# Pieces of W2's products in idle row quarters of the score visits, v passes that wait, zeros in early pauses, and a new plan

## The chip, the cores and the metric

The kernel runs on one core of a Trainium2 chip. The metric is the device time of one execution in microseconds (us). The core has a matrix engine (TensorE, here PE, with its weight loads PEld), a vector engine (DVE), a scalar engine (ACT), a general engine (POOL) and the queue that issues most DMAs (SP). They run side by side and wait for each other through semaphores.

## The reference

A block with 2048 tokens of 640 features mixes attention and a dense layer by a gate. In short:

```
qkv = x @ wqkv                       # 640 -> 3 * 640, 32 heads of 20
p   = softmax(q @ k.T * 20 ** -0.5)  # per head, 2048 x 2048
a   = (p @ v) @ wo
h   = x @ w1 + b1                    # 640 -> 1536
b   = (h * tanh(softplus(h))) @ w2   # 1536 -> 640
g   = sigmoid(sum(x * gate_w))
out = g * a + (1 - g) * b
```

The scores are the bulk: 32 heads x 2048 x 2048 exponentials.

## The kernel before

**Tiles.** Queries go in four chunks (c) of 512, heads in eight groups (g) of four (j = 0 to 3), keys in 16 tiles (kt) of 128. A unit (c, g, kt, j) is a score block of 128 keys by 512 queries; there are 2048. A head has 20 features, padded to 32 rows, so the product of a unit uses one 32-row quarter of PE's array, quarter j. Products in different quarters run beside each other (`score_mms`, L1294). All other products use all 128 rows and are cut into four column quarters of 32 (`quarters`, L532; `pv`, L1539), or use the whole array (`v_task`, `v_pair_task`, L853 and L880).

**Steps.** The main loop makes one exponential per step on ACT (`emit_e`, L1321), over two units, or three where `third` allows it. In the same step PE gets the scores of two steps later (`emit_s`): a visit of two or three units, to which `x_block` may add one whose exponential DVE makes. DVE converts that score block to an integer whose bits are a half float (L1379) and makes two shifted copies for each set of four (`piece`, L1409); the copies are weighted by scaled values V made on POOL (`weigh`, L1435). Such a set of four is called a tile here. After the scores, PE does passes with v (`emit_pv`: four heads at once, into bank ACC) and products of a task.

**Tasks.** Projections of K, Q and V, W1 (`h_task`, ten products), W2 (`b_task`: twelve products of 320 columns for 128 tokens and half of the features, 32 such tasks) and W_o (`p_task`) are `Task` objects, in a list in order of due times. One task at a time is open; `put` issues its products one after the other into one bank of PSUM, and the last product starts its eviction (`finish`). Banks 0 to 2 and 3 to 5 hold the scores of even and odd steps. Bank 6 is ACC. Banks 7, 5 and 2 are shared (`FLEX`): a third unit, a block for DVE or an open task takes one.

**The plan.** Everything is ordered when the kernel is built. `Plan` keeps an estimated clock per engine; `Plan.add` puts an instruction on an engine's list, with a cost, and charges SWITCH when PE changes between the kinds S (scores), V (v passes and column-quartered tasks) and F. The loop's choices compare these clocks with some thirty constants. STRETCHES gives other values for them from a step on, in 35 stretches. SHADE is the planned cost of a shifted copy. The finished lists run on the chip in that order, with semaphores only where one engine needs another's result.

**The start.** PE does six products of zeros into bank 5 and 7 (L599), turns the first 256 tokens by products with a unit matrix (`turn` in `first_keys`, L801), projects Q and K of head group 0 for them (`project`, L620), turns the next 256 tokens, and does the first scores. ACT and DVE copy results out of PSUM between these (L789, L790).

Of the kernel before, what the change touches and what calls it, by code (L numbers as in the profile page):

```python
# [49 lines left out]
SWITCH = 0.1025  # L50
# [93 lines left out]
SHADE = 0.61  # L144


EARLY = 0.35
SOON = 0.0
# [3 lines left out]
    13: {"CALM": 12, "CROWD": 1.22, "EAGER": 73, "FMIN": 0.198, "LATER": 0.157, "ROOM": 2.755, "SOON": 0.205, "SPUN": 0.607, "THIRD": 0.945, "VMIN": 1.27, "XSLACK": 0.224},  # L152
    33: {"AHEAD": 29, "BEHIND": 26.388, "CALM": 12, "CROWD": 1.22, "EAGER": 73, "FMIN": 0.198, "LATER": 0.157, "OVER": 0.17, "ROOM": 2.755, "SOON": 0.205, "SPUN": 0.607, "THIRD": 0.938, "VMIN": 1.398, "XSLACK": 0.37},
    53: {"AHEAD": 29, "BEHIND": 26.388, "BUSY": 0.647, "CALLED": 4.748, "CALM": 12, "CROWD": 1.22, "EAGER": 73, "EARLY": 0.551, "FMIN": 0.198, "KEPT": 12, "LATER": 0.157, "MARGIN": 0.809, "OVER": 0.17, "ROOM": 2.352, "SLACK": 0.261, "SOON": 0.092, "SPUN": 0.607, "THIRD": 0.938, "VMIN": 1.274, "XSLACK": 0.527},
    75: {"AHEAD": 29, "BEHIND": 15.903, "BUSY": 0.62, "CALLED": 4.748, "CALM": 12, "CROWD": 1.042, "EAGER": 83, "EARLY": 0.551, "FMIN": 0.122, "KEPT": 11, "LATER": 0.157, "MARGIN": 0.809, "OVER": 0.17, "PATIENCE": 7.416, "ROOM": 2.352, "SLACK": 0.261, "SOON": 0.092, "SPUN": 0.607, "STREAM": 0.537, "THIRD": 0.938, "VMIN": 1.274, "XSLACK": 0.527},
    97: {"AHEAD": 29, "BEHIND": 15.903, "BUSY": 0.62, "CALLED": 4.748, "CALM": 12, "CROWD": 1.042, "EAGER": 83, "EARLY": 0.551, "FMIN": 0.122, "KEPT": 11, "LATER": 0.157, "MARGIN": 0.809, "OVER": 0.17, "PATIENCE": 7.416, "ROOM": 2.352, "SLACK": 0.261, "SOON": 0.092, "SPUN": 0.607, "STREAM": 0.537, "THIRD": 0.938, "VMIN": 1.274, "XSLACK": 0.527},
    119: {"AHEAD": 29, "BEHIND": 15.903, "BUSY": 0.62, "CALLED": 4.748, "CALM": 12, "CROWD": 1.042, "EAGER": 83, "EARLY": 0.551, "FMIN": 0.122, "KEPT": 11, "LATER": 0.157, "MARGIN": 0.809, "OVER": 0.127, "PATIENCE": 7.416, "ROOM": 2.352, "SLACK": 0.261, "SOON": 0.092, "SPUN": 0.607, "STREAM": 0.537, "THIRD": 0.938, "VMIN": 1.274, "XSLACK": 0.527},
    141: {"BEHIND": 24.559, "CALLED": 1.144, "EARLY": 0.264, "KEPT": 12, "OVER": 0.186, "SPUN": 0.579},
    163: {"AHEAD": 21, "BEHIND": 24.496, "CALLED": 1.144, "CROWD": 0.988, "EARLY": 0.17, "KEPT": 12, "MARGIN": 0.364, "OVER": 0.186, "PATIENCE": 7.069, "ROOM": 2.123, "SPUN": 0.579, "VMIN": 0.687, "XLATE": 9.675},
    185: {"AHEAD": 21, "BEHIND": 24.496, "CALLED": 1.144, "CROWD": 0.988, "EARLY": 0.17, "KEPT": 12, "MARGIN": 0.364, "OVER": 0.26, "PATIENCE": 7.069, "ROOM": 2.123, "SPUN": 0.579, "STREAM": 0.336, "VMIN": 0.687, "XLATE": 9.675},  # L160
    205: {"AHEAD": 25, "BEHIND": 35.465, "CALLED": 0.932, "CROWD": 0.9, "EARLY": 0.172, "KEPT": 12, "MARGIN": 0.029, "OVER": 0.26, "PATIENCE": 3.704, "ROOM": 2.123, "SPUN": 0.579, "STREAM": 0.401, "VMIN": 0.687, "XLATE": 6.805, "XSLACK": 0.455},
    226: {"AHEAD": 25, "BEHIND": 35.465, "CALLED": 0.932, "CROWD": 0.9, "EARLY": 0.172, "KEPT": 12, "MARGIN": 0.029, "OVER": 0.26, "PATIENCE": 3.704, "ROOM": 2.123, "SOON": 0.261, "SPUN": 0.579, "STREAM": 0.401, "VMIN": 0.687, "XLATE": 6.805, "XSLACK": 0.612},
    247: {"AHEAD": 30, "BEHIND": 35.465, "CALLED": 0.932, "CROWD": 1.967, "EARLY": 0.172, "FMIN": 0.388, "FREE": 0.17, "KEPT": 12, "LATER": 0.621, "MARGIN": 0.029, "OVER": 0.322, "PATIENCE": 3.704, "ROOM": 2.123, "SOON": 0.261, "SPARED": 2, "SPUN": 0.579, "STREAM": 0.365, "VMIN": 0.687, "XLATE": 6.805, "XSLACK": 0.57},
    269: {"CALLED": 8.383, "SPUN": 0.576, "XSLACK": 0.465},
    288: {"CALLED": 8.383, "NEED": 6, "SPUN": 0.576, "XSLACK": 0.562},
    309: {"BEHIND": 23.94, "BUSY": 0.781, "CALLED": 8.383, "NEED": 6, "OVER": 0.396, "SPUN": 0.576, "THIRD": 0.444, "XSLACK": 0.562},
    329: {},
    351: {"BEHIND": 22.936, "BUSY": 0.732, "CROWD": 1.732, "EARLY": 0.305, "LOAD": 0.675, "OVER": 0.179, "PATIENCE": 2.889, "ROOM": 2.208, "VMIN": 0.705, "XLATE": 7.367, "XSLACK": 0.617},
    371: {"CALM": 7, "EARLY": 0.394, "MARGIN": 1.067, "SOON": 0.284, "STREAM": 0.467, "THIRD": 0.922},
    393: {"BEHIND": 28.654, "FMIN": 0.064, "LOAD": 0.638, "PATIENCE": 8.55, "VMIN": 0.653, "XSLACK": 0.487},  # L170
    413: {"MARGIN": 1.061, "SPUN": 0.615, "THIRD": 1.024, "XSLACK": 0.623},
    432: {"BUSY": 0.709, "CROWD": 0.989, "EARLY": 0.406, "FMIN": 0.123, "LATER": 0.297, "LOAD": 0.551, "MARGIN": 1.18, "OVER": 0.152},
    454: {"AHEAD": 38, "BUSY": 0.519, "CROWD": 0.989, "EAGER": 173, "EARLY": 0.406, "FMIN": 0.123, "LATER": 0.297, "LOAD": 0.551, "MARGIN": 1.161, "OVER": 0.152, "SPUN": 0.614, "STREAM": 0.359, "THIRD": 1.328, "VMIN": 1.002},
    474: {"AHEAD": 38, "BUSY": 0.807, "CALLED": 0.617, "CROWD": 0.989, "EAGER": 173, "EARLY": 0.406, "FMIN": 0.123, "LATER": 0.562, "LOAD": 0.551, "MARGIN": 1.161, "OVER": 0.152, "SPUN": 0.588, "STREAM": 0.359, "THIRD": 1.386, "VMIN": 1.939, "XSLACK": 0.252},
    494: {"BEHIND": 26.661, "BUSY": 0.707, "EAGER": 167, "MARGIN": 1.1, "PATIENCE": 3.566, "SPUN": 0.577, "STREAM": 0.513, "VMIN": 0.663, "XSLACK": 0.781},
    514: {},
    536: {"BUSY": 0.585, "CALLED": 2.393, "EARLY": 0.384, "FMIN": 0.098, "FREE": 0.232, "LOAD": 0.545, "MARGIN": 0.445, "PATIENCE": 6.193, "SLACK": 0.245, "STREAM": 0.457, "VMIN": 1.484, "XLATE": 7.039, "XSLACK": 0.513},
    556: {"SPARED": 1, "SPUN": 0.709, "STREAM": 0.531},
    577: {"BEHIND": 22.355, "EAGER": 146, "EARLY": 0.229, "LOAD": 0.461, "MARGIN": 1.156, "OVER": 0.132, "SPARED": 2, "SPUN": 0.709, "STREAM": 0.531, "XLATE": 9.211},
    598: {"BEHIND": 22.355, "EAGER": 63, "EARLY": 0.229, "FREE": 0.05, "KEPT": 15, "LOAD": 0.461, "MARGIN": 1.156, "NEED": 3, "OVER": 0.132, "SPARED": 2, "SPUN": 0.685, "STREAM": 0.531, "THIRD": 0.482, "VMIN": 0.813, "XLATE": 8.949},  # L180
    618: {"SPARED": 2, "THIRD": 0.433},
    639: {"BEHIND": 33.829, "BUSY": 0.336, "EAGER": 128, "SOON": 0.138, "SPARED": 2, "THIRD": 0.545, "XSLACK": 0.736},
    659: {"BEHIND": 33.719, "BUSY": 0.336, "CROWD": 1.058, "EAGER": 56, "FMIN": 0.095, "FREE": 0.212, "KEPT": 9, "LOAD": 0.71, "OVER": 0.155, "PATIENCE": 8.654, "SLACK": 0.168, "SOON": 0.138, "SPARED": 2, "SPUN": 0.63, "THIRD": 0.545, "XLATE": 2.946, "XSLACK": 0.366},
    680: {"BUSY": 0.499, "CROWD": 1.717, "LATER": 0.593, "MARGIN": 1.084, "NEED": 6, "OVER": 0.173, "PATIENCE": 8.859, "SPARED": 1, "SPUN": 0.559},
    702: {"BUSY": 0.71, "CALLED": 2.994, "EAGER": 176, "EARLY": 0.4, "FMIN": 0.091, "LATER": 0.47, "LOAD": 0.734, "ROOM": 2.176, "SPUN": 0.633, "XSLACK": 0.653},
# [12 lines left out]


class Plan:  # L200
# [1934 lines left out]
```

## Time and profile before

| | before |
|---|---|
| time, median of 3 runs | 744.35 us (743.04 to 745.58) |
| the profiled execution's own time | 744.41 us |
| its span, first to last instruction | 742.5 us |
| busy PE / DVE / ACT / POOL | 721.6 / 692.5 / 722.5 / 366.6 us |
| exponentials on ACT (L1321) | 736, 700.3 us busy |

A page of the profile gives the busy time of each engine, the chain of work that ended last, and groups of instructions by line: out<-in, the count, then busy time and mean duration in ns, then the idle time of the engine before them and what ended it. Consecutive instructions overlap by their latency, so the mean duration is longer than the step from one to the next. In a row of the timeline the first number is the start, the second the time from the first start to the last end of instructions merged into the row. In a row of waits the numbers are the total, the count and the longest.

### The profile page before, as it was taken

What the parts mean: (1) busy time and instruction counts of PE and PEld (TensorE: products, weight loads), DVE (VectorE), ACT (ScalarE), POOL (GpSimd) and SP (SyncE); (2) the same over time, 40 slices, a digit from 0 to 9 for tenths busy, and PEclk for the clock granted to TensorE, in tenths of its full rate; (3) what the DMA queues carried; (4) which work ended last, traced back from release to release, by engine and by line L of the source; (5) the groups of instructions that cost most, each with busy time, mean ns of one, the idle gap of its engine ahead of it and who ended that gap; (6) DMA issues with size and microseconds to landing.
All of it is one profiled execution on the core that took longest, in us unless ns stands there. A gap on an engine that the chain in (4) does not pass through costs nothing.

```text
span 742.5 us, 25540 instructions
## 1 busy us (share of the span) xinstructions
PE 721.6 (97%) x11013; PEld 272.2 (37%) x11016; DVE 692.5 (93%) x1203; ACT 722.5 (97%) x767; POOL 366.6 (49%) x705
## 2 busy tenths in 40 slices
PE   8999999999999999999999999999999999999996
PEld 4333333332333333332333334443333333433343
DVE  3799999999999998999899999999999999999985
ACT  6999999999999999999999999999999999999995
POOL 3303333062357635454234682668548766765531
PEclk9999999999999999999999999999999999999999
DMA  9312413212231324236321323131142121211111
GB/s 208 90 31 68 97 58 87 67 50 68 80 95 44 98 78 135 76 88 188 95 58 51 91 68 99 56 90 50 45 108 59 56 82 55 82 38 42 41 32 49
DMA packets 85125, 56.67 MB, mean 76 GB/s; under 512 B 22116, under 2 KB 80988, under 8 KB 85004
## 3 DMA queue, kind: packets, MB, share of 16 engines
q1 hardware_dynamic: 82636, 54.47, 26.3%
q8 instruction: 89, 1.46, 0.9%
q10 hardware_dynamic: 2256, 0.47, 0.3%
q14 instruction: 32, 0.26, 0.1%
q0 software_dynamic: 112, 0.01, 0.1%
HBM read 41.31 MB, written 12.83 MB: 73 GB/s over the span
## 4 chain that ended last, share of the span: by engine, by line
PE 45%; ACT 34%; DVE 15%; POOL 3%; DMA 1%; issue 1%; POOLq 0%
ACT ETS L1321 33%; PE PS L1294 16%; PE PS L1539 13%; PE PS L532 13%; DVE LN L1379 5%; DVE LN L1409 3%; PE PS L880 2%; POOL HB L1059 2%; DVE REG L1379 1%; DVE U L1058 1%; DVE HB L1019 1%; PE PS L620 1%; POOL U L1057 1%; DMA W2R<-in_B_w_dram 1%; DVE U L1062 1%
## 5 line engine op out<-in xcount | busy, mean ns | idle before, releaser
L1321 ACT ACTIVATE ETS<-PS 128x1024 bf16<-128x1024 f32 (+1 forms) x736 | 700.3, 1099 | 5.1 <-PE PS L1294 3.4
L1294 PE MATMUL PS<-QT,KT 32*128 32x512 bf16 (+1 forms) x2126 | 294.9, 377 | 9.9 <-ACT ETS L1321 6.4
L1379 DVE TENSOR_SCALAR LN<-PS 128x512 int16<-128x512 f32 x412 | 273.1, 681 | 11.2 <-PE PS L1294 10.4
L1435 POOL TENSOR_SCALAR VS<-V_all 128x84 bf16<-128x84 bf16 x278 | 156.0, 561 | 94.9 <-PE PS L1539 60.0
L1294 PEld LDWEIGHTS PS<-QT,KT 32*128 32x128 bf16 x2126 | 75.4, 91 | 233.6 <-ACT ETS L1321 180.5
L1539 PE MATMUL PS<-ETS,V_all 128*21 128x512 bf16 (+1 forms) x1564 | 145.5, 375 | 0.0
L1409 DVE TENSOR_SCALAR LN<-LN 128x2048 int16<-128x2048 int16 x192 | 138.8, 727 | 4.5 <-PE PS L1539 4.3
L1059 POOL TENSOR_TENSOR HB<-U,HB 128x128 bf16<-128x128 f16 x192 | 97.0, 539 | 86.1 <-DVE U L1058 86.1
L1603 POOL TENSOR_TENSOR QT<-OUNG,BCT 128x128 bf16<-128x128 f32 x124 | 60.8, 521 | 110.0 <-DMA BCT<-SUMS 110.0
L532 PE MATMUL PS<-XB,REG 128*32 128x256 bf16 (+1 forms) x1800 | 87.8, 296 | 0.5 <-DVE LN L1379 0.3
L1539 PE MATMUL PS<-LN,VS 128*21 128x512 f16 (+1 forms) x884 | 83.1, 378 | 0.2 <-DVE LN L1409 0.2
L532 PE MATMUL PS<-W2R,HB 128*32 128x320 bf16 x1536 | 76.0, 301 | 0.6 <-DVE LN L1379 0.4
L1539 PEld LDWEIGHTS PS<-ETS,V_all 128*21 128x21 bf16 x1564 | 37.8, 90 | 49.6 <-issue 40.7
L532 PEld LDWEIGHTS PS<-XB,REG 128*32 128x32 bf16 x1800 | 41.1, 95 | 28.6 <-issue 19.4
L1057 POOL TENSOR_SCALAR U<-REG 128x256 f16<-128x256 f32 x72 | 35.3, 515 | 27.4 <-ACT REG L1043 26.3
L532 PEld LDWEIGHTS PS<-W2R,HB 128*32 128x32 bf16 x1536 | 35.5, 96 | 25.9 <-issue 13.1
L1379 DVE TENSOR_SCALAR REG<-PS 128x512 int16<-128x512 f32 x60 | 40.1, 680 | 1.5 <-PE PS L1294 1.5
L1539 PE MATMUL PS<-LN,V_all 128*21 128x512 f16 (+1 forms) x424 | 40.2, 375 | 0.0
L532 PE MATMUL PS<-XB,WOQ 128*32 128x512 bf16 (+2 forms) x440 | 35.6, 382 | 0.2
L1539 PEld LDWEIGHTS PS<-LN,VS 128*21 128x21 bf16 x884 | 20.7, 89 | 41.0 <-issue 25.3
L532 PE MATMUL PS<-WOQ,QT 128*32 128x320 bf16 (+1 forms) x672 | 33.7, 301 | 1.2 <-DVE REG L1379 0.5
L1019 DVE TENSOR_TENSOR HB<-PS,B1F 128x512 bf16<-128x512 f32 x48 | 32.6, 680 | 1.0 <-PE PS L532 1.0
(117 smaller groups left out, 537.6 us busy)
## 6 DMA issues: line engine op xcount, KB each, us to landing
REG<-in_B_w_dram SPq DMA_DIRECT2D x36, 320.0 KB, 3.2
BCT<-SUMS SPq DMA_DIRECT2D x31, 256.0 KB
OT<-QT SPq DMA_DIRECT2D x30, 128.0 KB, 2.6
W2R<-in_B_w_dram SPq DMA_DIRECT2D x12, 320.0 KB, 5.0
QT<-QS SPq DMA_DIRECT2D x28, 128.0 KB, 4.0
KT<-KS SPq DMA_DIRECT2D x28, 128.0 KB
KS<-LN SPq DMA_DIRECT2D x16, 128.0 KB, 4.1
QS<-WOQ SPq DMA_DIRECT2D x16, 120.0 KB
```

The costliest lines, as they stand in the source:

```text
L532: last = e.matmul(to[at + j:at + j + n, :], w[:, j:j + n], x, start=start, stop=stop, tile_position=(0, at + j))
L880: return lambda e, bank: e.matmul(PS[:, bank, i * n:(i + 1) * n], xt(t // 4)[:, f, t % 4 * P:(t % 4 + 1) * P], WV[:, f, g * HD:g * HD + n] ...
L1019: ev = dve(lambda e: e.tensor_tensor(hb, PS[:, bank, :].rearrange("p (i t) -> p i t", i=2), bias, ALU.add), [last, *b1f, *guarded, *b_read ...
L1057: lift = lambda e, at: e.tensor_scalar(A[:, at], U[:, at], LIFT, LIFT, ALU.mult, ALU.add)
L1059: last = lambda e, at: e.tensor_tensor(h[:, at], A[:, at], h[:, at], ALU.mult)
L1294: op = pl.add("pe", lambda e, to=to, g=real(g), tile=tile, j=j, cols=cols, c=c, of_q=of_q: e.matmul(to[:, cols], KT[32 * j:32 * j + 32, g, ...
L1321: e_op[s] = pl.add("act", lambda e: e.activation(RING[:, p:p + n, :], scores(s)[:, 0:n, :], AF.Exp, scale=SCALE), [s_op[s], *(pv_slot[b] f ...
L1379: bank_free[bank] = x_ops[bank] = tile["op"] = dve(lambda e: e.tensor_scalar(dst, PS[:, bank, :], SCALE * ULPS, BASE, ALU.mult, ALU.add), ...
L1409: op = pl.add("dve", lambda e: e.tensor_scalar(to, src, SHADES[n] - SHADES[held], None, ALU.add), [made, *deps], cost=SHADE, lock=SHADE - ...
L1435: ops = [pl.add("pool", lambda e, i=i, n=n, src=src: e.tensor_scalar(VS[:, n, i, :, :], src, WEIGHTS[i + 1], None, ALU.mult), [v_done[(rea ...
L1539: lasts[n] = pl.add("pe", lambda e, v=v, j=j, src=src[:, cols], of_q=of_q, begin=begin, end=end: e.matmul(PS[32 * j:32 * j + EW, ACC, of_q ...
L1603: done = oung_free[m] = bc_read[0] = pl.add("pool", lambda e, some=some: e.tensor_tensor(otn(c, g)[:, some], src[:, some], BC[:, some], AL ...
```

## The change

- A `Task` may have `pair` products that it can give up. `beside` is called after the scores of a visit are on PE's list. Where an open task has enough products left (LEAVE), its last `pair` products are taken from its list and become four 32-row pieces each. In every visit one row that no score uses takes its piece, as a product of 32 rows and 128 output columns with its own tile position (`Row` in `quarters`), accumulating into the task's bank. One task gets one row per run of scores.
- A task whose other products are done before its pieces is parked: it keeps its bank (`held`), and the next task may open. `closed` starts the eviction after the last piece. `third`, `compose` and `home` respect such banks, and `block_of` prefers a block whose row no piece wants.
- While a task is open, v passes need `VOPEN` ready sets, not `VMIN`.
- `turn_over` adds products of zeros of 128 columns: six after the six of the start, three after the first transposes.
- SWITCH, SHADE and all 35 stretches have new values.

```diff
-SWITCH = 0.1025
+SWITCH = 0.1055
...
-SHADE = 0.61
+SHADE = 0.63
...
+LEAVE = 6
+LEFT = 100
+SPLITS = 1
+VOPEN = 1.5
...
 STRETCHES = {
...
-    723: {"BUSY": 0.71, "CALLED": 2.994, "EAGER": 45, "EARLY": 0.4, "FMIN": 0.29, "LATER": 0.47, "LOAD": 0.605, "MARGIN": 0.634, "OVER": 0.243, "ROOM": 2.176, "SOON": 0.057, "SPUN": 0.625, "XSLACK": 0.653},
...
+    491: {"AHEAD": 39, "BEHIND": 26.414, "BUSY": 0.932, "CROWD": 1.595, "EARLY": 0.355, "FREE": 0.135, "LATER": 0.554, "LEAVE": 2, "ROOM": 3.111, "SLACK": 0.116, "SOON": 0.258, "XLATE": 8.42, "XSLACK": 0.407},
...
+    720: {"CALLED": 5.425, "EARLY": 0.401, "FMIN": 0.154, "LOAD": 0.512, "OVER": 0.266, "SPARED": 1, "XLATE": 3.521},
 }
...
+        self.runs = 0
...
             if kind != self.kind:
                 at += SWITCH
                 self.kind = kind
+                self.runs += 1
...
+    def over(self):
+        return self.done == len(self.mms) and not any(left for _, left in self.parts)
...
         def quarters(e, to, w, x, start, stop, at=0):
 
+            if isinstance(e, Row):
+                if e.row is not None:
+                    some = slice(32 * e.row, 32 * e.row + 32)
+                    return e.e.matmul(to, w[some, :], x[some, :], start=False, stop=e.stop, tile_position=(32 * e.row, 0))
+                e, stop = e.e, stop or e.stop
...
             fn = task.mms[task.done]
             task.done += 1
-            op = pl.add("pe", lambda e: fn(e, bank), deps, cost=task.cost + MORE_MM, kind=task.kind)
-            if task.done == len(task.mms):
-                now["bank"] = True
-                bank_free[bank] = task.finish(bank, op)
-                now["bank"] = False
+            task.bank = bank
+            ends = task.pair and task.done == len(task.mms) and not any(left for _, left in task.parts)
+            op = pl.add("pe", lambda e: fn(Row(e, None, True) if ends else e, bank), deps, cost=task.cost + MORE_MM, kind=task.kind)
+            if task.over():
+                closed(task, op)
                 return True
             return False
+
+        def closed(task, op):
+
+            now["bank"] = True
+            bank_free[task.bank] = task.finish(task.bank, op)
+            now["bank"] = False
+
+        def wanted():
+
+            return {r for t in [*parked, *[now["open"]] * bool(now["open"])] for _, left in t.parts for r, _ in left}
+
+        def beside(units):
+
+            if not units or any(len(subs(*u[:3])) > 1 for u in units):
+                return
+            idle = [r for r in range(HG) if r not in {u[3] for u in units}]
+            for t in [*parked, *[now["open"]] * bool(now["open"])]:
+                if not t.pair or not idle:
+                    continue
+                rest = len(t.mms) - t.done
+                if not any(left for _, left in t.parts) and rest >= t.pair * (1 + LEAVE) and t.done >= t.after and t.split < SPLITS and len(order) > LEFT:
+                    t.split += 1
+                    t.parts.append((t.mms[-t.pair:], [(r, i) for r in range(HG) for i in range(t.pair)]))
+                    del t.mms[-t.pair:]
+                for fns, left in t.parts:
+                    rows = [r for r in idle if any(v[0] == r for v in left)]
+                    if not rows:
+                        continue
+                    if t.run == pl.runs:
+                        break
+                    t.run = pl.runs
+                    some = [v for v in left if v[0] == rows[0]]
+                    for v in some:
+                        left.remove(v)
+                        idle = [r for r in idle if r != v[0]]
+                        op = pl.add("pe", lambda e, v=v, fns=fns, t=t, stop=t.over(): fns[v[1]](Row(e, v[0], stop), t.bank),
+                                    [t.beside], cost=0.004, kind="S")
+                    t.beside = op
+                    break
+                if t.over():
+                    closed(t, op)
+                    if t in parked:
+                        parked.remove(t)
+                        del held[t.bank]
+                    else:
+                        now["open"] = None
+                    ended_task(t)
...
+            def turn_over(n):
+
+                for _ in range(n):
+                    pl.add("pe", lambda e: e.matmul(
+                        PS[:, ACC, 0:P], RING[:, 0, 0:P], RING[:, 0, 0:P], start=True, stop=True), [m_zero], cost=0.0)
+
+            turn_over(6)
...
                 bank_free[3] = turn(0, [4], 3, "dve")
+                turn_over(3)
...
+                return Task([mm(f) for f in range(NFT)], PASS, finish, due, lambda: [*xt_load[c], w_load["wk"]], True, pair=1)
...
+                return Task([mm(f) for f in range(NFT)], PASS, finish, due, lambda: [*xt_load[c], w_load["wq"]], True, pair=int(m == P))
...
+                            dve=WIDE + MISH, pair=2, after=NFT + 1)
...
-                return Task([mm(f) for f in range(NFC)], HALF * COL, finish, due, ready)
+                return Task([mm(f) for f in range(NFC)], HALF * COL, finish, due, ready, pair=1)
...
-            return Task([p_mm(c, t, half, g, some) for g in some], HALF * COL, finish, due, ready)
+            return Task([p_mm(c, t, half, g, some) for g in some], HALF * COL, finish, due, ready, pair=int(fast and c < NC - 1))
...
-            if not fast or s < CALM or x and x[2] == bank or now["open"] and now["home"] == bank or now["rate"] >= CALLED:
+            if not fast or s < CALM or bank in held or x and x[2] == bank or now["open"] and now["home"] == bank or now["rate"] >= CALLED:
...
-            j = next((j for j in tile["left"] if j not in js), tile["left"][0])
+            need = wanted()
+            j = min(tile["left"], key=lambda j: (j in js, j in need))
...
             if issue(task, now["home"]):
                 now["open"] = None
+                ended_task(task)
+            elif task.done == len(task.mms):
+                now["open"] = None
+                parked.append(task)
+                held[task.bank] = "parked"
...
                 emit_s(step + 2)
+                if fast:
+                    beside([*slots[step + 2], *(x[1:2] if x else ())])
...
-            if tight or sets() >= VMIN:
+            if tight or sets() >= (VOPEN if now["open"] else VMIN):
```

More of the change, by code (lines that the diff above doesn't have):

```diff
@@ L163 @@
[L163 to L166, printed above, removed]
@@ L291, with __init__ @@
 class Task:
-    def __init__(self, mms, cost, finish, due, ready=None, forced=False, dve=HALVED, kind="V"):
+    def __init__(self, mms, cost, finish, due, ready=None, forced=False, dve=HALVED, kind="V", pair=0, after=1):
+        self.after, self.pair, self.parts, self.bank, self.split, self.run, self.beside = after, pair, [], None, 0, -1, None
         self.mms, self.cost, self.finish, self.due, self.forced, self.dve = mms, cost, finish, due, forced, dve
@@ L1871, in fill_up @@
                 free = bank_free.get(bank)
-                idle = not now["open"] and (free is None or free.t1 + HOP <= pl.now["pe"])
+                idle = not now["open"] and bank is not None and (free is None or free.t1 + HOP <= pl.now["pe"])
                 if idle and last and pl.now["pe"] + PASS <= upto:
```

98 lines of the change are left out of this document (54 added, 44 removed).

## The prediction

> **What bounds the kernel now.** I read the page first: busy times, the chain that ended last, the costliest groups.
>
> ```profile
> PE 721.6 (97%) x11013; PEld 272.2 (37%) x11016; DVE 692.5 (93%) x1203; ACT 722.5 (97%) x767; POOL 366.6 (49%) x705
> ...
> PE 45%; ACT 34%; DVE 15%; POOL 3%; DMA 1%; issue 1%; POOLq 0%
> ...
> L1379 DVE TENSOR_SCALAR LN<-PS 128x512 int16<-128x512 f32 x412 | 273.1, 681 | 11.2 <-PE PS L1294 10.4
> ...
> L1409 DVE TENSOR_SCALAR LN<-LN 128x2048 int16<-128x2048 int16 x192 | 138.8, 727 | 4.5 <-PE PS L1539 4.3
> ...
> L532 PE MATMUL PS<-W2R,HB 128*32 128x320 bf16 x1536 | 76.0, 301 | 0.6 <-DVE LN L1379 0.4
> ```
>
> Three engines are nearly full, so the share of busy time decides nothing. The question is what ACT loses, because the exponentials (L1321) are a load that runs nearly from the start to the end. The groups of ACT between 20 and 720 us, and then three rows of ACT's timeline:
>
> ```profile
> L1321 ACT ACTIVATE ETS<-PS 128x1024 bf16<-128x1024 f32 x682 | 640.2, 1077 | 4.0 <-PE PS L1294 2.5 <-PE PS L1539 0.4
> L1321 ACT ACTIVATE ETS<-PS 128x1536 bf16<-128x1536 f32 x32 | 48.3, 1514 | 0.3 <-PE PS L1294 0.3
> L1043 ACT ACTIVATE REG<-HB 128x1024 f32<-128x1024 bf16 x18 | 20.1, 1116 | 0.0
> L1043 ACT ACTIVATE W2R<-HB 128x1024 f32<-128x1024 bf16 x6 | 6.5, 1080 | 0.0
> ```
> ```profile
> 659.52 11.13 ACT L1321 ACTIVATE ETS<-PS 128x1024 bf16<-128x1024 f32 x12
> 670.49 1.10 ACT L1043 ACTIVATE REG<-HB 128x1024 f32<-128x1024 bf16 x1
> 671.44 51.27 ACT L1321 ACTIVATE ETS<-PS 128x1024 bf16<-128x1024 f32 x54
> ```
>
> Instructions overlap by their latency, so the undisturbed step comes from the run of twelve pairs: (11.13 - 1.08)/11 = 0.914 us. A tanh (L1043) takes 671.44 - 670.49 = 0.95 us. A triple takes 1.35 us (a pair and 1.514 - 1.077 = 0.44 more). 682 x 0.914 + 32 x 1.35 + 24 x 0.95 = 689.3 of the 700 us. **In 700 us ACT loses 10.7 us** to late scores. A new order of the same work can win no more there. More than that needs fewer units on ACT: a unit of 512 columns costs half a pair, 0.457 us, and a tile that DVE takes over frees four, 1.83 us.
>
> The start is the other place. The chain of waits in order of time, up to 13 us, then the same rows in the timeline:
>
> ```profile
> 0.73 3.63 DMA LN<-in_A_x_dram
> ...
> 4.41 0.62 PE PS L801 x4
> ...
> 5.05 0.70 DVE XB L790
> ...
> 5.80 2.31 PE PS L620 x40
> 8.12 1.18 PE PS L801 x10
> 9.30 0.55 PE PS L1294 x8
> ```
> ```profile
> 1.19 2.74 PE L599 MATMUL PS<-ETS 128*128 128x512 bf16 x6 [1.19 <-DVE ETS L587]
> ...
> 4.41 1.25 PE L801 MATMUL PS<-LN 128*128 128x128 bf16 x10 [0.48 <-DMA LN<-in_A_x_dram]
> ...
> 6.83 1.28 PE L620 MATMUL PS<-XB,REG 128*20 128x256 bf16 x20
> ...
> 8.17 0.37 ACT L789 CAST KT<-PS 128x256 bf16<-128x256 f32 x1 [2.10 <-PE PS L620]
> ...
> 9.23 0.62 PE L1294 MATMUL PS<-QT,KT 32*128 32x256 bf16 x8
> ...
> 9.88 4.84 ACT L1321 ACTIVATE ETS<-PS 128x1024 bf16<-128x1024 f32 x5 [0.60 <-PE PS L1294]
> ...
> 11.69 0.72 PE L620 MATMUL PS<-XB,REG 128*20 128x256 bf16 x20
> ```
>
> Five projection passes (L620 x20) take 1.28 us at 6.83 but 0.72 us at 11.69: the same instruction at half and at full speed, while the granted clock reads 1.00. So until about 10 us TensorE runs at half rate, and PE stands on the chain from 5.80 to the first exponential with nothing but one copy beside it.
>
> **The change, part by part.** The sum is made against the profiled execution, 744.41 us (span 742.5 and 1.9 around it); the median of the runs is 744.35, so the two stand for each other.
>
> Zeros in early pauses. Six 128-column products follow the six warm-up ones, three more follow the first transposes. At half rate a 128-column product takes (1.25 - 0.31)/9 = 0.10 us (an estimate; the 0.31 is the last one's latency), so 0.6 and 0.3 us. They lie beside the load of x's rows (lands at 0.73 + 3.63 = 4.36) and beside DVE's copy (to 5.76); PE idles 0.48 and 0.14 us there by the rows, 0.2 more each if the drain of the product before counts. If the rows land early, they cost at most 0.2 us. What they bring is an earlier full rate. If it came by 5.80, 40 projection passes of 20 instructions each save 0.56 twice (K ends near 7.0, not 8.1), ten transposes need 0.5 instead of 1.1 us, the copy of K (0.37) runs beside them, scores start near 7.6 and take 0.2 less: first exponential 1.8 us earlier. If it came only at 8.0, transposes and scores save 0.75. If it comes as now, 0. I take 1.3, the middle of the two cases with an effect, as the trace turned to full rate about 4.4 us after the last real pause (5.80 to 10.2), and that pause would be gone. No DMA stands on the chain after 4.36, and ACT loses 10.7 of 700 us behind it, so this reaches the end. **-1.3 (-1.8 to +0.2).**
>
> The Trainium skill ("TensorE: Matmul & The Clock Gate", Part 1) says that the array leaves half rate after one busy window of about 3.4 us, and that this window runs free of the kernel's start. The trace agrees as far as it goes: 2.7 us of warm-up, then pauses, did not do it. By the page the estimate for a busy stretch from 1.19 is 4.6 to 8.0 us, hence a term between -0.75 and -1.8, but it also speaks against the change: with a lucky window the old kernel would be quick at about 7.9 us too.
>
> Pieces of W2's products. In the code a task gives up its last product only with LEAVE (5 to 7) times as many left; K tasks have 5 products and W1 tasks ten in two halves, so only W2's 32 tasks of 12 split, and a few of W_o's in the one stretch with LEAVE 2. The rows of one such task and of the scores around it:
>
> ```profile
> 452.46 0.39 PE L1294 MATMUL PS<-QT,KT 32*128 32x512 bf16 x3
> 452.78 0.59 PE L532 MATMUL PS<-W2R,HB 128*32 128x320 bf16 x12
> 453.30 0.45 PE L1294 MATMUL PS<-QT,KT 32*128 32x512 bf16 x3
> 453.68 0.73 PE L532 MATMUL PS<-W2R,HB 128*32 128x320 bf16 x16
> 454.34 0.39 PE L1294 MATMUL PS<-QT,KT 32*128 32x512 bf16 x3
> 454.66 0.86 PE L532 MATMUL PS<-W2R,HB 128*32 128x320 bf16 x20
> ```
>
> One product is 0.73 - 0.59 = 0.14 us; 32 of them are 4.5 us of PE. The four quarters ride in visits with three rows in use; their 320 columns are shorter than the scores' 512, so they lie beside them and end first. What reaches the end is the part where PE, not ACT, comes last. From the waits between 20 and 720 us:
>
> ```profile
> PEld PS L1294 <- ACT ETS L1321: 173.9, 483, 1.1
> ...
> DVE LN L1379 <- PE PS L1294: 10.4, 31, 2.5
> ...
> DVE LN L1409 <- PE PS L1539: 4.3, 11, 1.1
> ```
>
> ACT releases the scores in 483 of 714 visits; in the other third a shorter PE helps: 0.32 x 4.5 = 1.4 at most, none if all saved time falls in the 483. **-0.7 (-1.4 to 0;** the loss side is the third rival).
>
> VOPEN, SHADE, SWITCH and the new stretches. The wait of the v passes is one of the planner, not a semaphore: while a projection is open they need two ready sets. Behind a late pass wait the reuse of its line by DVE (4.3 us in all now) and the scaling of V on POOL, half idle; doubling the DVE one would cost 4.3. The new constants stand closer to the rows. Scores at 454.34 to W2 at 454.66 is 0.32, of which 512 columns stream for 0.21: a switch of 0.107, planned 0.1025, now 0.1055. A shade shows 138.8/192 = 0.72 busy, an eviction 273.1/412 = 0.66 where 0.60 is planned; less the same 0.06 the shade is 0.66, planned 0.61, now 0.63. So the plan sees some 192 x 0.02 = 4 us of DVE's lateness that it did not see. What an order can do is bounded by the stages of now, first 60 to 260, then 560 to 660 us:
>
> ```profile
> L1321 ACT ACTIVATE ETS<-PS 128x1024 bf16<-128x1024 f32 x209 | 193.8, 1097 | 0.2 <-PE PS L1294 0.2
> L1321 ACT ACTIVATE ETS<-PS 128x1536 bf16<-128x1536 f32 x4 | 6.0, 1507 | 0.0
> L1043 ACT ACTIVATE W2R<-HB 128x1024 f32<-128x1024 bf16 x3 | 3.3, 1111 | 0.0
> ```
> ```profile
> L1321 ACT ACTIVATE ETS<-PS 128x1024 bf16<-128x1024 f32 x100 | 94.1, 1052 | 1.7 <-PE PS L1294 1.0 <-PE PS L1539 0.4
> L1043 ACT ACTIVATE REG<-HB 128x1024 f32<-128x1024 bf16 x7 | 7.5, 1070 | 0.0
> ```
>
> The first loses 200 - 209 x 0.914 - 4 x 1.35 - 3 x 0.95 = 0.7, the second 100 - 100 x 0.914 - 7 x 0.95 = 2.0. All 700 us like the first would lose 2.5 (8.2 less than now), all like the second 14 (3 more). I take **-1.0 (-8.2 to +4.3)**, a tenth of the loss, near no change: the truer constants speak for a gain, but a new plan also puts new collisions where the old one had none.
>
> 744.41 - 1.3 - 0.7 - 1.0 = **741.4 us**. What follows the last exponential does not change: no product splits within the last 100 units.
>
> **The rivals.** First, the plan wins more: half of ACT's 10.7 us goes. For it: the later stages, where W2's products run, lose most (2.0 in 100 us above, against 0.7 in 200). Against it: DVE has no less to do. 744.41 - 1.3 - 0.7 - 5.3 = 737.1.
>
> Second, the change does little: full rate comes as now because the pauses did not decide, and the saved PE time falls where PE waits for ACT. For it: 483 waits for ACT. Against it: the pauses are the only break between 1.19 and 9.3 us. 744.41 - 0 - 0.3 - 0.4 = 743.7.
>
> Third, slower: parked tasks hold banks. One row of a task is placed per visit (the planner's check on runs), so four quarters need four visits, some 3.7 us, where the rows above show twelve products done in three visits. Of the three banks for evictions (7, 5, 2) one is then taken longer, fewer blocks find one, and tiles go back from DVE to ACT at 1.83 us each. The Trainium skill ("TensorEngine Tiling", Gotcha 1) states that different row tiles cannot use one PSUM bank at once; no run here shows it, and it is the reason that this can't be shortened. Against it: DVE is the limit for tiles, as it waits for scores only 10.4 us in 31 places. It decides from the third lost tile on, since zeros and pieces win 2.0 us and 2.2 more would still count as no change: (2.0 + 2.2)/1.83 = 2.3. With three tiles the time is 744.41 - 2.0 + 5.5 = 747.9.
>
> **How the numbers follow.** This kernel's measurement can tell 0.3% (2.2 us) from no change: faster is below 742.1, slower above 746.6. The forecast has 0.42 (its own range 738.5 to 742.1), the first rival 0.13, the second 0.25, the third 0.20. The forecast and the first give faster, 0.55; the second the same, 0.25; the third slower, 0.20. The range 737.0 to 746.5 leaves out about half of the first rival's lower side (0.05) and most of the third (0.15).
>
> **What would show it.** Zeros: L620 x20 near 0.72 instead of 1.28 us before 8 us, and the first L1321 at 8.1 to 9.1 us. If L1321 starts at 9.8, term one fails. Pieces: W2R,HB products of 128x32 fall from 1536 to about 1408, and some 128 of 32x128 with 320 columns appear beside scores. Plan: the lost time of ACT between 20 and 720 us, worked out as above, at 8 to 10 us. Third rival: fewer evictions on L1379 (412 into LN now) and more units on L1321. A first exponential that moves while the end does not would mean that ACT is held further on by something the chain does not show.

## The result, and the profile after

The changed kernel takes 748.29 us (median of 7 runs, 746.43 to 749.49), the kernel before beside it 744.35 us (743.04 to 745.58). The ratio is 1.0057 [1.0044, 1.0069]: slower by 0.6%, where 741.4 was forecast and 746.5 was the upper end of the range. The profiled execution took 747.88 us with a span of 746.1, so it is 3.5 us longer than the profiled one of before (744.41).

The page of the kernel after, its busy times, the granted clock, the chain that ended last and three groups:

```profile
PE 717.2 (96%) x11005; PEld 270.2 (36%) x11008; DVE 686.9 (92%) x1191; ACT 723.6 (97%) x762; POOL 356.4 (48%) x699
...
PEclk9999999899999999999999999999999999999999
...
ACT 63%; PE 28%; DVE 6%; DMA 2%; issue 1%; ACTq 0%; DVEq 0%
...
L1459 DVE TENSOR_SCALAR LN<-PS 128x512 int16<-128x512 f32 x420 | 277.6, 678 | 8.5 <-PE PS L1374 7.4
...
L1489 DVE TENSOR_SCALAR LN<-LN 128x2048 int16<-128x2048 int16 x192 | 137.7, 719 | 10.1 <-PE PS L1620 9.7
...
L555 PE MATMUL PS<-W2R,HB 128*32 128x320 bf16 x1436 | 72.0, 301 | 0.0
```

PE and DVE have 4 to 6 us less to do, ACT 1.1 us more. One digit of the granted clock, the eighth slice of 18.65 us (131 to 149 us), is an 8 in a row of nines. It turns out to be the place that matters.

**Did each part do what the diff says?** The start, from the timeline of the kernel after:

```profile
3.72 0.85 PE L676 MATMUL PS<-ETS 128*128 128x128 bf16 x6
...
5.67 0.53 PE L676 MATMUL PS<-ETS 128*128 128x128 bf16 x3
6.13 1.17 PE L698 MATMUL PS<-XB,WOQ 128*20 128x256 bf16 x20
7.13 0.72 PE L698 MATMUL PS<-XB,REG 128*20 128x256 bf16 x20
...
8.87 1.94 ACT L1401 ACTIVATE ETS<-PS 128x1024 bf16<-128x1024 f32 x2 [0.18 <-PE PS L1374]
```

The nine zero products are there; five projection passes take 0.72 us at 7.13, so the array is at full rate there (10.3 before), and the first exponential starts at 8.87 instead of 9.88.

A visit with a piece, from PE's timeline of the same kernel at 382 us, and the group of pieces:

```profile
381.98 0.39 PE L1374 MATMUL PS<-QT,KT 32*128 32x512 bf16 x2
381.98 0.31 PE L551 MATMUL PS<-W2R,HB 32*128 32x320 bf16 x1
381.99 0.38 PE L1374 MATMUL PS<-QT,KT 32*128 32x512 bf16 x1
```
```profile
L551 PE MATMUL PS<-W2R,HB 32*128 32x320 bf16 x100 | 29.3, 305 | 0.0
```

The piece streams beside the three scores and ends before them. Over the whole trace a visit of three scores followed by other work occupies PE for 0.325 us with a piece (median of 75) and 0.322 us without (425): a piece costs some 3 ns. 25 tasks were split, 100 pieces for 100 fewer products of 128*32 (1536 to 1436, four instructions to a product).

**What ACT has to do.** Groups of the exponentials by shape over the whole span, first before, then after:

```profile
L1321 ACT ACTIVATE ETS<-PS 128x1024 bf16<-128x1024 f32 x700 | 657.8, 1077 | 4.7 <-PE PS L1294 3.1 <-PE PS L1539 0.6
L1321 ACT ACTIVATE ETS<-PS 128x1536 bf16<-128x1536 f32 x36 | 54.6, 1521 | 0.3 <-PE PS L1294 0.3
```
```profile
L1401 ACT ACTIVATE ETS<-PS 128x1024 bf16<-128x1024 f32 x677 | 637.9, 1099 | 7.5 <-PE PS L1374 6.4 <-PE PS L1620 0.2
L1401 ACT ACTIVATE ETS<-PS 128x1536 bf16<-128x1536 f32 x54 | 82.6, 1536 | 0.5 <-PE PS L1374 0.4
```

1508 units before (1400 + 108), 1516 after (1354 + 162). Eight units, two tiles, went from DVE to ACT. With the prediction's steps the load is 700 x 0.914 + 36 x 1.35 = 688.4 us before and 677 x 0.914 + 54 x 1.35 = 691.7 after: 3.3 us more.

**What ACT loses.** The same groups after, between 20 and 720 us:

```profile
L1401 ACT ACTIVATE ETS<-PS 128x1024 bf16<-128x1024 f32 x656 | 617.6, 1101 | 6.8 <-PE PS L1374 5.8
L1401 ACT ACTIVATE ETS<-PS 128x1536 bf16<-128x1536 f32 x49 | 75.1, 1538 | 0.5 <-PE PS L1374 0.4
L1122 ACT ACTIVATE REG<-HB 128x1024 f32<-128x1024 bf16 x18 | 19.9, 1103 | 0.0
L1122 ACT ACTIVATE W2R<-HB 128x1024 f32<-128x1024 bf16 x6 | 7.0, 1163 | 0.0
```

700 - 656 x 0.914 - 49 x 1.35 - 24 x 0.95 = 11.5 us, against 10.7 before. But it lies elsewhere. The waits of the kernel after between 131 and 146 us alone:

```profile
ACT ETS L1401 <- PE PS L1374: 5.0, 3, 3.7
DVE RR L1753 <- DMA RR<-OUNG: 3.8, 1, 3.8
...
PE PS L1374 <- DVE LN L1459: 2.8, 1, 2.8
```

Five of the 11.5 us are lost in one place. Outside it ACT loses 6.5 us, 4.2 less than before. **Without that one stop the new order loses much less; with it, it loses as much as the old one and has 3.3 us more to do.** What happens there, from the timeline of the kernel after, DVE's and SP's rows first:

```profile
123.69 0.68 DVE L1746 COPY OUNG<-PS 128x512 f32<-128x512 f32 x1
125.09 0.47 SPq L756 DMA_DIRECT2D KS<-LN  x1
125.61 0.85 SPq L748 DMA_DIRECT2D QS<-ZEROS  x1
130.07 1.06 SPq L772 DMA_DIRECT2D KT<-KS  x2
131.18 0.55 SPq L1749 DMA_DIRECT2D RR<-OUNG  x1
...
135.17 0.39 PE L1374 MATMUL PS<-QT,KT 32*128 32x512 bf16 x2
137.48 0.25 DVE L1753 RECIPROCAL RR<-RR 128x16 f32<-128x16 f32 x1 [3.77 <-DMA RR<-OUNG]
137.65 0.63 DVE L1459 TENSOR_SCALAR LN<-PS 128x512 int16<-128x512 f32 x1
...
138.33 0.60 PE L1374 MATMUL PS<-QT,KT 32*128 32x512 bf16 x1 [2.77 <-DVE LN L1459]
...
140.54 1.02 ACT L1401 ACTIVATE ETS<-PS 128x1024 bf16<-128x1024 f32 x1 [3.68 <-PE PS L1374]
```

It reads from top to bottom. DVE has the row sums of the fifth head group in OUNG at 124.37. The load that brings them back as RR issues only at 131.18, 6.8 us later, because it stands on SP's queue behind two fetches of K (KT<-KS), and these wait for K's write (KS<-LN, issued at 125.09). DVE comes to the reciprocal (L1753) at 133.7 and stands 3.77 us. Behind it on DVE waits an eviction (L1459); its score bank is not free, so PE waits 2.77 us with the next scores (L1374); without them ACT waits 3.68 us, then twice more. The sums load itself, from issue to landing, stands in the chain of waits:

```profile
131.18 6.27 DMA RR<-OUNG
```

At each of the other 30 group ends the load issues at most 3.5 us after the copy. Windows of the kernel after; the columns are the busy time and count of PE, PEld, DVE, ACT, POOL, then the granted clock, the DMA share and GB/s:

```profile
136.00:144.00 8.00, 5.67 (x42) 1.80 (x43) 5.25 (x10) 3.02 (x4) 0.00 (x0) 0.57 0.16 44
144.00:160.00 16.00, 16.00 (x186) 6.58 (x182) 14.43 (x27) 16.00 (x18) 4.21 (x10) 1.00 0.26 64
```

Behind PE's pause the array falls to half rate (0.57 granted; scores take 0.60 instead of 0.39 us) until 143.6, which delays the next scores as well.

### The profile page after: what moved, and what is told of

The parts are those of the page before. It is cut to its first block, busy times and chain, and to the rows that moved or that the text cites. A ratio compares the mean times of both kernels' runs of the same rounds, so it can differ in the third digit from the quotient of the medians.

```text
span 746.1 us, 25504 instructions
## 1 busy us (share of the span) xinstructions
PE 717.2 (96%) x11005; PEld 270.2 (36%) x11008; DVE 686.9 (92%) x1191; ACT 723.6 (97%) x762; POOL 356.4 (48%) x699
## 4 chain that ended last, share of the span: by engine, by line
ACT 63%; PE 28%; DVE 6%; DMA 2%; issue 1%; ACTq 0%; DVEq 0%
ACT ETS L1401 61%; PE PS L1374 10%; PE PS L1620 9%; PE PS L555 7%; DVE LN L1459 2%; ACT REG L1122 2%; DVE LN L1489 1%; PE PS L959 1%; PE PS L698 1%; DMA RR<-OUNG 1%; DMA QS<-WOQ 1%; DMA LN<-in_A_x_dram 1%; PE PS L932 0%; DVE WOQ L835 0%; DVE HB L1218 0%
## 5 line engine op out<-in xcount | busy, mean ns | idle before, releaser
L1374 PE MATMUL PS<-QT,KT 32*128 32x512 bf16 (+1 forms) x2126 | 293.6, 378 | 17.0 <-ACT ETS L1401 11.0
L1459 DVE TENSOR_SCALAR LN<-PS 128x512 int16<-128x512 f32 x420 | 277.6, 678 | 8.5 <-PE PS L1374 7.4
L1515 POOL TENSOR_SCALAR VS<-V_all 128x84 bf16<-128x84 bf16 x272 | 151.9, 558 | 89.5 <-PE PS L1620 59.5
L1374 PEld LDWEIGHTS PS<-QT,KT 32*128 32x128 bf16 x2126 | 75.4, 91 | 245.0 <-ACT ETS L1401 209.7
L1620 PE MATMUL PS<-ETS,V_all 128*21 128x512 bf16 (+1 forms) x1576 | 144.9, 375 | 0.1
L1138 POOL TENSOR_TENSOR HB<-U,HB 128x128 bf16<-128x128 f16 x192 | 94.2, 523 | 86.8 <-DVE U L1137 86.8
L1620 PE MATMUL PS<-LN,VS 128*21 128x512 f16 (+1 forms) x848 | 81.4, 382 | 0.9 <-DVE LN L1489 0.9
L555 PE MATMUL PS<-W2R,HB 128*32 128x320 bf16 x1436 | 72.0, 301 | 0.0
L1136 POOL TENSOR_SCALAR U<-REG 128x256 f16<-128x256 f32 x72 | 33.2, 483 | 32.5 <-ACT REG L1122 31.1
L555 PEld LDWEIGHTS PS<-W2R,HB 128*32 128x32 bf16 x1436 | 32.6, 96 | 24.1 <-issue 13.7
L1459 DVE TENSOR_SCALAR REG<-PS 128x512 int16<-128x512 f32 x52 | 34.8, 679 | 0.8 <-PE PS L1374 0.6
```

The source lines that it names most:

```text
L555: last = e.matmul(to[at + j:at + j + n, :], w[:, j:j + n], x, start=start, stop=stop, tile_position=(0, at + j))
L1136: lift = lambda e, at: e.tensor_scalar(A[:, at], U[:, at], LIFT, LIFT, ALU.mult, ALU.add)
L1138: last = lambda e, at: e.tensor_tensor(h[:, at], A[:, at], h[:, at], ALU.mult)
L1374: op = pl.add("pe", lambda e, to=to, g=real(g), tile=tile, j=j, cols=cols, c=c, of_q=of_q: e.matmul(to[:, cols], KT[32 * j:32 * j + 32, g, ...
L1459: bank_free[bank] = x_ops[bank] = tile["op"] = dve(lambda e: e.tensor_scalar(dst, PS[:, bank, :], SCALE * ULPS, BASE, ALU.mult, ALU.add), ...
L1515: ops = [pl.add("pool", lambda e, i=i, n=n, src=src: e.tensor_scalar(VS[:, n, i, :, :], src, WEIGHTS[i + 1], None, ALU.mult), [v_done[(rea ...
```

## The experiments

None of these kernels leaves any of the computation out. Ratios are to the kernel before on the same chip.

**Each new part alone, and the suspected write moved.** First the zeros alone in the kernel before, and the changed kernel without them:

```diff
...
+            turn_over(6)
...
+                turn_over(3)
```

> The kernel before with the nine products of zeros and nothing else; the order of all other work is the same. First theory: the full rate comes some 3 us earlier and the first exponential at about 8.9 us instead of 9.9, and this reaches the end: 743.3 us (-1.0). Rival: ACT is held later by the loads of the other chunks of x and gives the microsecond back: 744.4.

743.32 us against 743.08, ratio 1.0004 [0.9995, 1.0013]. The zeros alone gain nothing that can be told; the expected 1.0 us fell.

> The changed kernel without its nine products of zeros, all else in the same order. First theory: the first exponential goes back to about 9.9 us and the time to 749.3 (+1.0 on 748.3). Rival (the stop at 131 to 144 us depends on how early the work before it is): the stop shrinks when the start is late, and the time stays at 748.3 or falls below.

745.56 us against 743.08, ratio 1.0022 [1.0012, 1.0032]. The kernel did not become slower without the zeros, so the 749.3 of the first theory fell. The stop is there without the zeros too, with a shorter wait of DVE (2.7 us): the array is at half rate from 138.1 to 144.9.

Then the blanking of Q's padding for the third chunk (QS<-ZEROS, issued at 125.61 after), issued after step 46 instead of 112. The planner still charges it at 112, so that all else keeps its order:

```diff
...
-            later(112, lambda: clear(2))
+            later(46, lambda: clear_now(2))
+            later(112, lambda: clear_planned(2))
```

> The changed kernel with one DMA moved: the blanking of the padding rows of Q's third chunk (QS<-ZEROS) is issued after step 46 instead of step 112; the planner still charges it at step 112, so nothing else moves. First theory (the stop): at 125 us this transfer delays the write of K, the queue behind it and with it the load of the row sums, DVE waits for it, PE idles and its clock halves, and ACT loses 5.3 us there; without it 743.0 us (742.5 to 744). Rival (the load): the eight more units on ACT and the order as such set the time, and a stop that goes here comes back as other waits: 747 to 748.5.

741.42 us against 743.08, ratio 0.9977 [0.9969, 0.9986]. K's write is followed by no blanking now. The sums load still stands behind the two fetches and issues at 130.22, 6.15 us after the copy, but it lands sooner, as its row in the chain of waits tells:

```profile
130.22 4.27 DMA RR<-OUNG
```

4.27 us from issue to landing, where it was 6.27. The reciprocal waits only 1.1 us and the array stays at full rate. The stop is the loss. That the traffic of the blanking lengthens the load's way by 2.0 us fits this; what the order on the queue has to do with it, this run doesn't tell.

Then the pieces: the same order, but each of the 25 last products done whole where it stood, and the pieces left out:

```diff
+            if task.parts and task.done == len(task.mms):
+                fns = task.parts[0][0]
+                op.fn = lambda e: [f(e, bank) for f in [fn, *fns]][-1]
...
+    fast.ops = [o for o in fast.ops if o.piece is None]
...
```

> The changed kernel in the same order, but the last product of each of the 25 split tasks is done whole on 128 rows right behind the one before it, and the 100 pieces beside scores are left out. First theory: PE gets 25 x 0.14 = 3.5 us longer, a third of it where PE comes last: 748.3 + 0.5 (0 to 1.2). Rival (pieces lengthen the visits or hold banks): -0.5 or more below 748.3.

746.93 us against 743.08, ratio 1.0050 [1.0037, 1.0063]. Taking the pieces out does not bring the time back: they are not what slows the kernel. The profiled execution is the quickest of its five (744.34 us, the others 746.1 to 747.8). In it the reciprocal waits 2.0 us and the array keeps its full rate, so the stop is not the same in every run.

**The order on the queue.** The changed kernel once more, beside the next three on one chip:

> The changed kernel once more, beside the other three on one chip. The first measurement gave 1.0057 of the kernel before; on this chip that is about 4 us above it. It is the reference for the three below.

745.75 us against 743.38, ratio 1.0023 [1.0008, 1.0037]. That is 2.4 us above the kernel before, where some 4 were expected. Its twelve runs go from 742.27 to 748.52 us, and the longer ones have the lower granted clock (0.999 in the two shortest, 0.990 in the longest). In its profile the reciprocal waits 3.7 us and the array is at half rate from 136.8 to 143.6, as in the first one.

The sums load of the fifth group is put ahead of the two fetches that wait, and the blanking stays where it was:

```diff
+    sums = [o for o in fast.ops if o.slot == "nr0"][4]
+    n = fast.ops.index(sums)
+    late = [o for o in fast.ops[:n] if o.eng == "sp"][-2:]
...
+    fast.ops = [o for o in fast.ops[:n] if o not in late] + [sums, *late] + fast.ops[n + 1:]
```

> The changed kernel with the blanking left at step 112, but the load of the row sums (RR<-OUNG) is put on the queue ahead of the two fetches of K that wait for K's write. If the stop comes from the order on the queue (the load stands behind fetches that wait), it goes: about 6 us less than the changed kernel, near a_clear46. If it comes from the traffic of the blanking itself, the load still lands late and the time stays within 2 us of the changed kernel.

741.34 us (740.84 to 742.27) against 743.38, ratio 0.9972 [0.9963, 0.9981], and 4.4 us below the changed kernel on the same chip. SP's rows in its timeline, and its groups of exponentials between 20 and 720 us:

```profile
124.96 0.56 SPq L1749 DMA_DIRECT2D RR<-OUNG  x1
128.12 1.06 SPq L772 DMA_DIRECT2D KT<-KS  x2
```
```profile
L1401 ACT ACTIVATE ETS<-PS 128x1024 bf16<-128x1024 f32 x661 | 621.5, 1102 | 1.7 <-PE PS L1374 0.8
L1401 ACT ACTIVATE ETS<-PS 128x1536 bf16<-128x1536 f32 x50 | 76.3, 1533 | 0.5 <-PE PS L1374 0.4
```

The load changed places with the two fetches, and DVE waits for no sums any more. ACT loses 700 - 661 x 0.914 - 50 x 1.35 - 24 x 0.95 = 5.5 us, half of what the kernel before loses. The blanking alone does not make the stop. In the new plan the order alone does not make it either, as the run with the blanking moved had the same order and a wait of 1.1 us. The stop there needs both: the load behind the two fetches, and the blanking ahead of them.

Now the counterpart, the same order in the kernel before: the two next fetches of K put ahead of its fifth sums load, and nothing else changed.

```diff
...
+    ahead = [o for o in fast.ops[n + 1:] if o.eng == "sp"][:2]
...
+    fast.ops = fast.ops[:n] + ahead + [o for o in fast.ops[n:] if o not in ahead]
```

> The kernel before, with one change of order on the queue: the two fetches of K that wait until 133.6 us for K's write are put ahead of the load of the fifth row sums, which is issued at 126.7 us now. Everything else keeps its order. Theory (a load of sums behind a waiting fetch stops DVE): the load is issued at about 134.7 and lands near 140, DVE reaches its reciprocal at 134.1 and waits 4 to 6 us, the clock halves and the time rises by 4 to 7 us over the kernel before. Rival (the stop belongs to the new plan, where PE had just run out of other work): DVE waits but most of it is caught up, 0 to 2 us.

750.63 us against 743.65, ratio 1.0093 [1.0080, 1.0107]: 7.0 us from two DMAs ahead of a third. SP's rows in the timeline of the kernel before, then of this one, and its waits from 125 to 150 us:

```profile
126.70 0.63 SPq L1668 DMA_DIRECT2D RR<-OUNG  x1
133.62 1.06 SPq L694 DMA_DIRECT2D KT<-KS  x2
```
```profile
131.97 1.07 SPq L694 DMA_DIRECT2D KT<-KS  x2
133.09 0.55 SPq L1668 DMA_DIRECT2D RR<-OUNG  x1
```
```profile
ACT ETS L1321 <- PE PS L1294: 7.2, 4, 5.6
DVE RR L1672 <- DMA RR<-OUNG: 5.1, 1, 5.1
```

All links come back in the old kernel: the late load, DVE at the reciprocal, ACT without scores, and half rate (138.5 to 145.4 us). Here the load issues 9.6 us after the copy (123.50) and lands 4.5 us later, so the order alone is enough. In the old kernel the stop is shown to follow from the place of one load on a queue that issues in order.

**What zeros and pieces are worth with the stop mended.** On the kernel with the blanking at 46, once without the zeros and once with whole products:

> As a_clear46 (the blanking moved to step 46, no stop at 131 us), without the nine products of zeros. Theory after the first four runs: the array's activity window runs free of the kernel's start, so the full rate comes early in many runs without zeros too, and zeros are worth 0 to 0.5 us on average: 741.4 to 742. Rival one (the zeros are worth the 1.0 us that the two first profiles show): 742.4. Rival two (zeros cost, as the changed kernel without them was 2.6 us faster): 739 to 740.

743.23 us against 743.38, ratio 0.9999 [0.9987, 1.0011]; with zeros it is 0.9977. That is on the side of the first rival, with 1.6 us for the zeros. But three of its twelve runs took 745.0 to 745.6 us, two of them at a granted clock of 0.995 where nine have 0.997 to 0.999, so the array may have been at half rate for longer in these; none of them was traced.

> As a_clear46, and the last products of the 25 split tasks are done whole, the 100 pieces left out, the order else the same. Theory: the pieces save 25 x 0.14 = 3.5 us of PE, of which a third at most comes last: whole products cost 0.5 (0 to 1.2): 741.9. Rival (pieces hinder): 740.5 or less.

742.37 us against 743.38, ratio 0.9987 [0.9977, 0.9997]; with pieces it is 0.9977. And pieces without the new plan: the kernel before with the zeros and, in 20 of its 32 W2 tasks, the last product replaced by pieces in four visits between its other products.

```diff
+    def split_up(pl):
...
+    split_up(fast)
```

> The kernel before with the zeros, in its own order, with pieces: 20 of W2's 32 tasks have four visits with the four idle rows between their first and last product; there the last product is replaced by four pieces, one in each visit. No bank is held longer. Theory: 20 x 0.14 = 2.8 us of PE saved, a third of it where PE comes last: 0.3 to 0.9 us below the kernel with zeros alone (743.3 on its chip, 1.0004 of the kernel before). Rival (pieces are worth nothing without a new plan): the same as with zeros alone.

742.43 us against 743.65, ratio 0.9984 [0.9973, 0.9994]; with the zeros alone it is 1.0004.

Two differences tell what pieces bring: 0.0010 x 743 = 0.7 us, and 0.0020 x 743 = 1.5 us. Each is uncertain by 1.0 us (both intervals combined); together they are 1.1 us, uncertain by 0.7. For the zeros the changed kernel itself tells nothing, as its stop varies more (1.0022 without them, 1.0057 and 1.0023 with them). There remain +0.3 us (0.7 either way) in the old order and -1.6 (1.1) with the stop mended. These lie 1.9 us apart, more than the 1.3 that both intervals allow, so they are not averaged: what the zeros are worth is not settled.

**The start of the kernel before, once more.**

> The kernel before once more, for a second look at its start. If the activity window runs free of the start, the full rate comes at another time than 10.3 us (anywhere from 5 to 11) and the first exponential moves with it, between 8 and 10 us; if it is fixed by the pauses, both stay at 10.3 and 9.9.

743.2 us, and the start is not that of the first profile. Two rows of its timeline:

```profile
5.40 0.72 PE L620 MATMUL PS<-XB,WOQ 128*20 128x256 bf16 x20 [0.45 <-DVE XB L790]
...
8.03 1.94 ACT L1321 ACTIVATE ETS<-PS 128x1024 bf16<-128x1024 f32 x2 [0.18 <-PE PS L1294]
```

The same kernel that ran its projections at half rate until about 10 us has them at full rate from 5.40 here (the granted clock turns at 4.1, earlier than the 5 to 11 expected) and starts its exponentials 1.85 us earlier.

**Both mends together.** The changed kernel with the sums load ahead of the fetches and the blanking at 46:

> The changed kernel with both mends: the load of the row sums ahead of the two waiting fetches, and the blanking issued after step 46. If each of them removes the whole stop, both together give what the better one gives, 0.9972 of the kernel before (741.3); if the traffic of the blanking still costs something elsewhere, 0.5 to 1 us less than that.

741.14 us (740.8 to 741.4) against 743.65, ratio 0.9963 [0.9951, 0.9975]. By the ratios that is 0.7 us below the better mend alone, with 1.1 us either way, so whether the blanking costs anything else is not decided. This beats both kernels, and its runs spread over 0.6 us where those of the changed kernel spread over 6.3.

## Why the prediction was wrong

**What bounds the kernel: right, and it found the stop.** ACT's loss, worked out from the count of its instructions, was the right quantity. Where it was lost by place, the stop stood out at once, though the page shows 97% busy ACT in both kernels.

**Zeros, -1.3 forecast: sized on one late start.** The mechanism is there, and the marker looked confirmed: 0.72 us before 8 us, first exponential at 8.87. But the marker compared with a single start of the kernel before that was a late one. Five profiles of kernels without zeros reach full rate at 10.3, 4.1, 5.0 (and lose it again from 11.8 to 15.2), 9.4 and 5.4 us; their first exponentials start at 9.88, 8.03, 8.08, 9.67 and 8.00, 8.7 on average. Nine with zeros reach it at 4.4 to 7.1 and start at 8.08 to 8.87. The thirteenth exponential ends at 21.6 and 21.1 us on average: in these few profiles the zeros remove the late starts, and that is worth 0.5 us. Of the measured times the one in the old order (+0.3, 0.7 either way) leaves no room for -1.3, the one with the stop mended (-1.6, 1.1 either way) does. The prediction had named the reason that speaks against the change, from the Trainium skill ("TensorE: Matmul & The Clock Gate", Part 1: the window runs free of the kernel's start, so with a lucky one the old kernel is quick too), and then gave it no weight. The five starts bear that rule out.

**Pieces, -0.7 forecast: right.** They bring 1.1 us with 0.7 either way; four pieces of some 3 ns on PE stand in for a product of 0.14 us. 25 tasks were split instead of 32.

**VOPEN, SHADE, SWITCH and the new stretches, -1.0 (-8.2 to +4.3) forecast: this is the step that failed.** It took the loss of the new plan to lie between those of two stages of the old one, all 700 us like the best or like the worst. Both are smooth stages, and two things are in neither.

- The stop. The new order put two waiting fetches ahead of the sums load, and the blanking ahead of them lengthened the load's way. It costs ACT 5.0 us in the profile and 4.4 us of the time on the same chip (745.75 to 741.34). The prediction asked only of the v passes what is queued behind them and never went through SP's queue, where the order was new too. Its sentence "a new plan also puts new collisions where the old one had none" was the right thought, without a price. The old trace had the row for one: the load of the fifth group issues 6.9 us ahead of the fetches (126.70 and 133.62), and its landing was in time for the reciprocal at 134.07. Put behind them, it costs 7.0 us, as the experiment shows, which is outside the +4.3.
- The load. The term counted only what an order can lose, with "the same work". The new plan left eight more units on ACT, 3.3 us, and that was no part of the sum (only the third rival had a price for lost tiles).

Against these stands what the new plan wins: ACT loses 5.5 instead of 10.7 us once the stop is gone. In the profiled execution: +3.3 of load, +0.8 of loss (11.5 less 10.7), -1.0 at the start (8.87 less 9.88) make +3.1 of the 3.5 us measured. With the sums load ahead: +3.3 - 5.2 - 1.8 (its first exponential starts at 8.08) = -3.7, where its profiled execution of 741.10 is 3.3 below that of before, taken on another chip and with its late start.

**The rivals.** The first (the plan wins more) has its mechanism, half of the loss gone, hidden under the stop and the eight units. The second (little change) falls. The third gave 747.9 us, near the 748.29, with a marker that came true in part (two tiles lost, where it decides from three), but its cause is not what the runs show: without the stop the kernel is faster than before with all its tasks parked as planned, and with the stop it is slower even where the pieces are left out. Its other marker, fewer than 412 evictions into LN, came out as 420, since tiles into other buffers fell instead (1508 units on ACT mean 540 blocks on DVE, 1516 mean 532). Why the new plan gives two tiles back was not tried.

**The last line of the forecast's markers** held: the first exponential moved by 1.0 us and the end did not follow, because ACT was held further on. The chain of the whole run did show it: 2% of DMA, where it was 1%.

Open: how much of the stop is PE's half rate. Of the 5.0 us, 3.7 is the first wait; the two later ones (0.82 and 0.48 in the timeline) and slower products behind them are an argued 1.3 to 2 us. Products to keep the array busy in the pause were not tried. Nor is it shown why the stop differs between runs of one kernel, or what the zeros are worth.

## What to carry to other kernels

When an order is planned anew, go through each in-order queue, the DMA queue first: for every load that an engine will stand at, ask what waits in front of it on that queue, for what, and how much time the trace leaves until it is needed. An average loss from smooth stages is no bound for that; here one load behind two waiting fetches cost 4.4 and 7.0 us, more than the 3.0 us that the whole change was forecast to win. And before a term is built on the start of one profile, look at a second one of the same kernel.

## What the runs showed of the hardware

- **Half rate in the middle of a kernel.** Pauses of PE of 1.66, 2.7, 2.77 and 4.5 us at the scores were each followed by 6.8 us at half rate (138.1 to 144.9, 136.8 to 143.6 twice, 138.5 to 145.4); one of 1.02 us was not. What sorts them is the share of the 3.4 us before the fall in which the array streamed, worked out from the columns of the products in the trace: 0.35, 0.42, 0.42 and 0.02 before the four falls; in the body of all these kernels no other such stretch is below 0.43. As the trace misses some products, the limit is only roughly placed. At the start it doesn't sort as well: without the zeros the array fell back to half rate at 11.8 us after a share of about 0.47. The Trainium skill ("TensorE: Matmul & The Clock Gate", "Why this matters for your kernels") warns of idle gaps over about 3 us between bursts of products; here a gap of 1.66 us with thin work around it was enough.
- **The window runs free.** In the kernel after, full rate at 7.1 us and half rate at 136.8 are 129.7 us apart, 38 x 3.413, and the half rate lasts 2 x 3.413: the falls and returns lie on one grid. A grid that starts anywhere would also explain (argued, not shown) why the same kernel gets its full rate at 10.3 us in one execution and at 4.1 in another. The shares fit this: worked out as above, the stretch of the grid that ended with full rate had 0.74 or more in all 14 starts, and the ones before it 0.73 or less.
- **Work in an idle quarter of the array is nearly free in this kernel:** some 3 ns for a piece of 32 rows and 320 columns beside three scores of 512.
